# Moving the attention values, their transposes, the masking and the FFN subtractions in the issue order of a fused top-k attention and FFN kernel

## Chip, cores and metric

The kernel runs on one core of a Trainium2 chip. The metric is the device time in microseconds of one execution, as the median of several runs. The core has five engines with a queue each, and each works through its queue in order: PE (matmuls, with weight loads as PEld), DVE (vector), ACT (activations and copies), POOL (element by element), and SP, which here only issues DMAs.

## The reference, cut to what matters

```python
# q, k, v: (8, 8, 576, 64) float32
scores = np.matmul(q, k.transpose(0, 1, 3, 2)) / 8.0
kth = np.partition(scores, -32, axis=-1)[..., -32:-31]
scores = np.where(scores >= kth, scores, -1e9)
attn = np.exp(scores - scores.max(-1, keepdims=True))
attn = attn / (attn.sum(-1, keepdims=True) + 1e-09)
x = np.matmul(attn, v)                                   # back to (4608, 512)
h = x @ w_in                                             # 512 -> 2048
out = (h - np.tanh(h)) @ w_out                           # 2048 -> 512
```

So each row of 576 scores keeps its 32 largest, these go through a softmax, and the attention output feeds a two-layer network (the FFN below). w_in and w_out come as float64; the kernel converts them to float32 itself.

## The kernel before

The work is cut into 144 **steps**. A step is 128 query rows (`qt`) of a pair of heads (`hp`) of one batch (`b`), both heads `t` side by side. Four `qt` cover 512 of a batch's 576 rows; the last 64 rows of two neighbouring head pairs make a "rem" step. Steps stand in **groups** of up to two `qt` with the same heads, and what follows the softmax is done once per group. The rows of all heads together feed a **unit** of the FFN: 256 rows ("xT"), or 128 left-over rows of two batches ("xTr").

What happens to step n, and on which engine:

- `scores(n)`: matmuls (L237, PE) into the one PSUM tile `scps`, then a copy to `sc` (L245, ACT). The two heads use the two halves of the array's rows.
- `search(n, ...)`: DVE finds the 32 largest. It first merges the halves of each row (L267, L268: reads `scps` and `sc`, writes `ab`, two buffers), then takes four rounds of max and match_replace (L270 to L278). Between the rounds `between(i)` issues other DVE work: turning k and q (L222), the reciprocals of the sums (L345), the turn of an earlier `z` (L376), and pieces of the weights' conversion.
- `mask(n, ...)`: POOL makes the threshold `tb` (L294) and the bias `nb` (L303) from `m`; for each head ACT makes a Relu (L307) and POOL subtracts it from the scores (L310), which gives `z`. Last come the row checks `bad` (L314, POOL), the last readers of `ab`: they find rows in which the fast search could be wrong.
- `expo(n)`: two exponentials with their row sums (L330, ACT), then `rd` (L340, POOL).
- The probabilities have to be turned for the product with v. For the first batch this is done by `turn_pe` ("pe" steps): nine PE transposes (L409) and ACT copies to `et` (L412), eight transposes in a first part and one in a second. For all others DVE turns blocks (L376) and 16 DMAs per group on SP spread them into `et` (L390). `et` has one buffer.
- `spread(n)` copies the inverted sums to `rx` (L355, POOL).
- `values(n)`: twenty matmuls in pairs per normal group (L433, PE; the two heads use the two halves of the array's columns), then one transpose of `rx` for each step of the group (L441, PE) into the same PSUM tile `av`. ACT copies it to `xs` (L445), and POOL multiplies the two parts into the unit's `xT` (L457, or L448 for left-over rows). If this completes a unit, the unit's FFN items join the list `work`.

The FFN items are `ffn_h` (L486: x times w_in; every second one has tanh L498, copy L499 on ACT and the subtraction L500 on POOL, giving `g`) and `ffn_o` (L507: two matmuls of g times w_out; every eighth copies to `ot`, L517, and stores). The tiles `th`, `ot` and the conversion's `f` share four buffers.

The conversion of the weights (`convert`) runs in the first steps: DVE L157, L163 and L169, ACT L158, L161 and L166, POOL L172.

The order of all this is written out by hand. The loop at the end of `run` takes one pass per step n and issues, in this order: `spread(n-3)`; `values` of a group that is due (three or four steps old); `rate()`, which sets how many FFN items this pass may take from `work`; the first part of `turn_pe(n-2)`; `mask(n-1)`; `search(n)`; the DMAs of `spread_keys(n-2)`; `deal(0.4)`, which issues that share of the items; `scores(n+1)`; the second part of `turn_pe`; `expo(n-1)`; `deal(0.2)`; `values(n-2)` for pe steps; `deal(0.2)`; loads; `deal(0.2)`. After all steps the rest of `work` is issued. `rate()` spreads the items now in `work` over the passes to the next completed unit:

```python
have, low, high = len(work), 0.0, None
coming = sorted((t, u.n // 8) for u, t in ready.items() if t > n)
for t, k in coming + [(NS + 4, 0)]:
    r = have / max(t - n, 1)
    high = r if high is None else min(high, r)
    have += k
```

At the end of the kernel a flag is computed from `bad`; only if it is set does an exact second run follow. It is not executed with these inputs.

Of the kernel before, what the change touches and what calls it, by code (L numbers as in the profile page):

```python
# [8 lines left out]
AF = mybir.ActivationFunctionType  # L9
ALU = mybir.AluOpType  # L10
FP32 = mybir.dt.float32
# [5 lines left out]
BIG = 2.0**80  # L17
# [31 lines left out]
def kernel(  # L49
# [9 lines left out]
    nc = tc.nc  # L59
    P = nc.NUM_PARTITIONS  # L60
    B, H, S, D = q.shape
# [9 lines left out]
    NG = P // G  # L71
    KC = 2 * S // P
    G = 32
    NG = P // G
# [17 lines left out]
    zpool = pool("z", 2)  # L92
# [191 lines left out]
    def mask(n, exact):  # L284

        x = st[n]
        sc, m = x["sc"], x.pop("m")
        scf = sc[:].rearrange("p t s k -> p t (s k)")
        tb = mpool.tile([P, 2], FP32, tag="tb", name="tb")
        if exact:  # L290
            nc.gpsimd.tensor_scalar(tb[:], m[:, :, TOP - 1], BIG, None, ALU.mult)
        else:
            for t in range(2):
                nc.gpsimd.tensor_scalar(  # L294
                    tb[:, t : t + 1],
                    m[:, t, TOP - 1 : TOP],
                    m[:, t, TOP - 9 : TOP - 8],
                    BIG,
                    ALU.min,
                    ALU.mult,  # L300
                )
        nb = mpool.tile([P, 2], FP32, tag="nb", name="nb")
        nc.gpsimd.tensor_scalar(nb[:], m[:, :, 0], -scale, None, ALU.mult)  # L303
        z = zpool.tile([P, 2 * S], FP32, tag="z", name="z")
        zv = z[:].rearrange("p (t k) -> p t k", t=2)
        for t in range(2):
            nc.scalar.activation(  # L307
                zv[:, t, :], scf[:, t, :], AF.Relu, bias=tb[:, t : t + 1], scale=-BIG
            )
            nc.gpsimd.tensor_tensor(zv[:, t, :], scf[:, t, :], zv[:, t, :], ALU.subtract)  # L310
        if not exact:
            ab = x.pop("ab")
            for t in range(2):
                nc.gpsimd.tensor_scalar(  # L314
                    bad[:, t, n : n + 1],
                    ab[:, t, S2 + 7 : S2 + 8],
                    BIG,
                    tb[:, t : t + 1],
                    ALU.mult,
                    ALU.is_gt,  # L320
                )
        x.update(z=z, zv=zv, nb=nb)

    rds = {}
# [94 lines left out]
    def values(n):  # L419

        g = steps[n]
        nq, u = g.nq, g.unit
        et = tiles(ets.pop(n), nq)
        rx = rxs.pop(n)
        w = nq * P
        av = zt_ps.tile([P, 2, N], FP32, tag="zt", name="av")
        for i in range(2 if g.rem else 1):
            cols = half(i) if g.rem else slice(0, w)
            es = et[:, 2 * i : 2 * i + 2] if g.rem else et
            hp = g.hp + i  # L430
            for c in range(J + 1):
                for t in range(2):
                    nc.tensor.matmul(  # L433
                        av[half(t), 0, cols],
                        vb[g.b, hp][:, t, c, :] if c < J else vr[g.b, hp][:, t, :],
                        es[:, :, (J + 1) * t + c if c < J else J].rearrange("p a i j -> p a (i j)"),
                        start=(c == 0),
                        stop=(c == J),
                    )
        for i in range(nq):  # L440
            nc.tensor.transpose(  # L441
                av[:, 1, 0:w].rearrange("p (a i j) -> p i a j", a=NG, i=nq)[:, i], rx[:, i].rearrange("p t d -> p (t d)"), ident[:]
            )
        xs = xrpool.tile([P, 2, N], FP32, tag="xs", name="xs")
        nc.scalar.copy(xs[:, :, 0:w], av[:, :, 0:w])  # L445
        if g.rem:
            for i in range(2):
                nc.gpsimd.tensor_tensor(  # L448
                    xt(u)[:, g.hp + i, g.col : g.col + R],
                    xs[:, 0, half(i)],  # L450
                    xs[:, 1, half(i)],
                    ALU.mult,
                )
        else:

            xv = xs[:, :, 0:w].rearrange("p s (a i j) -> p s i a j", a=NG, i=nq)
            nc.gpsimd.tensor_tensor(  # L457
                xt(u)[:, g.hp, g.col : g.col + w].rearrange("p (i a j) -> p i a j", a=NG, i=nq),
                xv[:, 0],
                xv[:, 1],  # L460
                ALU.mult,
            )
        if n in done:
            work.extend(ffn(u))
# [6 lines left out]
            u.xT = p.tile([P, CD, N], FP32, tag=u.tag, name=u.tag)  # L471
        return u.xT

    cur = {}

    def ffn_h(u, item):

        w = u.n
        per = 2 * P // w
        for f in range(item * per, (item + 1) * per):  # L480
            j, fo = f // FJ, (f % FJ) * P
            s = f * w % 512
            if s == 0:
                cur[u] = h_ps.tile([P, 512], FP32, tag="h", name="hps")
            for c in range(CD):
                nc.tensor.matmul(  # L486
                    cur[u][:, s : s + w],
                    w_in[j][:, c, fo : fo + P],
                    u.xT[:, c, 0:w],
                    start=(c == 0),  # L490
                    stop=(c == CD - 1),
                )
        if item % 2:
            th = thpool.tile([P, 512], FP32, tag="th", name="th")
            if item % 4 == 1:
                u.g.append(gpool.tile([P, 2, 512], FP32, tag="g", name="g"))
            g = u.g[-1][:, item % 4 // 2, :]
            nc.scalar.activation(th[:], cur[u][:], AF.Tanh)  # L498
            nc.scalar.copy(g, cur[u][:])  # L499
            nc.gpsimd.tensor_tensor(g, g, th[:], ALU.subtract)  # L500

    def ffn_o(u, i, part):
        if part == 0:
            cur[u] = h_ps.tile([P, DM], FP32, tag="h", name="ops")
        for f in range(2 * part, 2 * part + 2):
            o = f * u.n + i * P
            nc.tensor.matmul(  # L507
                cur[u][:],
                u.g[o // 1024][:, o % 1024 // 512, o % 512 : o % 512 + P],
                w_out[f // FJ][:, f % FJ, :],  # L510
                start=(f == 0),
                stop=(f == CF - 1),
            )
        if part < CF // 2 - 1:
            return
        ot = thpool.tile([P, DM], FP32, tag="th", name="ot")
        nc.scalar.copy(ot[:], cur[u][:])  # L517
        for rows, dst in u.blocks[i]:
            nc.sync.dma_start(dst, ot[rows, :])
# [50 lines left out]
    def run(exact):  # L570
# [67 lines left out]
        def here(i):  # L638
            return 0 <= n + i < NS
# [24 lines left out]
        def rate():  # L664
# [8 lines that stand above are left out]
            for u, t in begun.items():  # L673
                if t > n and u in before:
                    need = [i + 1 for i, x in enumerate(work) if x[1] is before[u]]
                    if need:
                        low = max(low, need[-1] / (t - n))
            return max(low, high)
# [11 lines left out]
        for n in range(-4, NS + 4):  # L690
            pe = here(-2) and steps[n - 2].pe
            if here(-3) and not steps[n - 3].pe:
                spread(n - 3)
            for m in (n - 4, n - 3):
                if 0 <= m < NS and steps[m].last and steps[m].lag == n - m:
                    values(m)
            share, usable = rate(), converted[0]
            if pe:
                w = turn_pe(n - 2)
                next(w)  # L700
            if here(-1):
                mask(n - 1, exact)
            if here(0):
                search(n, exact, between)
            elif here(-2):
                between(0)
            if here(-2) and not pe and steps[n - 2].last:
                spread_keys(n - 2)
            if pe:
                spread(n - 2)  # L710
            deal(0.4)
            if here(1):
                scores(n + 1)
            if pe:
                next(w)
            if here(-1):
                expo(n - 1)
            deal(0.2)
            if pe and steps[n - 2].last:
                values(n - 2)  # L720
            deal(0.2)
            for fn in todo.pop(n, []):
                fn()
            deal(0.2)
# [48 lines left out]
```

## Time and profile before

| what | value |
|---|---|
| median of 5 runs | 1547.95 us (1546.23 to 1551.09) |
| the profiled execution's own time | 1551.75 us |
| its span in the profile | 1549.9 us |
| PE busy | 1442.3 us, 93% |
| DVE busy | 1347.3 us, 87% |
| ACT busy | 883.1 us, 57% |
| POOL busy | 941.4 us, 61% |
| granted PE clock, mean | 0.975 |

The page cuts the span into 40 slices and shows each engine's busy share in tenths and the granted clock of PE likewise. A group row names line, engine, operation, tiles and shape, then the time in all and the mean of one. A timeline row gives start, length of a merged run of equal instructions, engine, line, operation, and in brackets the idle time ahead and what ended it. A row of waits says who waited for whom: microseconds in total, times, longest. A row of stretches gives each engine's busy time in a window, with instructions in brackets, then clock, DMA share and rate. Ends of matmuls are modelled, and matmuls overlap; the distance from the start of one to the start of the next is measured.

### The profile page before, as it was taken

What the parts mean: (1) busy time and instruction counts of PE and PEld (TensorE: products, weight loads), DVE (VectorE), ACT (ScalarE), POOL (GpSimd) and SP (SyncE); (2) the same over time, 40 slices, a digit from 0 to 9 for tenths busy, and PEclk for the clock granted to TensorE, in tenths of its full rate; (3) what the DMA queues carried; (4) which work ended last, traced back from release to release, by engine and by line L of the source; (5) the groups of instructions that cost most, each with busy time, mean ns of one, the idle gap of its engine ahead of it and who ended that gap; (6) DMA issues with size and microseconds to landing.
All of it is one profiled execution on the core that took longest, in us unless ns stands there. A gap on an engine that the chain in (4) does not pass through costs nothing.

```text
span 1549.9 us, 25298 instructions
## 1 busy us (share of the span) xinstructions
PE 1442.3 (93%) x7428; PEld 913.1 (59%) x7428; DVE 1347.3 (87%) x3828; ACT 883.1 (57%) x1567; POOL 941.4 (61%) x1525
## 2 busy tenths in 40 slices
PE   2566899899999999999999999999999999999997
PEld 1355467456565665656565665656566665656673
DVE  7987889999999999999999999999999999997300
ACT  4886767556565565656555565656565565655320
POOL 3777667667565675657565675757565675746420
PEclk9777899999999999999999999999999999999999
DMA  9944113324443354334443354234443345322200
GB/s 248 361 167 157 50 28 66 91 69 93 106 92 76 82 105 103 70 79 95 103 89 76 81 105 103 70 79 97 102 89 80 81 99 110 81 64 59 73 10 16
DMA packets 258835, 147.42 MB, mean 95 GB/s; under 512 B 210048, under 2 KB 217216, under 8 KB 258688
## 3 DMA queue, kind: packets, MB, share of 16 engines
q1 hardware_dynamic: 256912, 145.49, 38.4%
q8 instruction: 62, 1.02, 0.3%
q14 instruction: 85, 0.70, 0.2%
q10 hardware_dynamic: 1776, 0.22, 0.1%
HBM read 61.85 MB, written 9.44 MB: 46 GB/s over the span
## 4 chain that ended last, share of the span: by engine, by line
PE 73%; DVE 10%; SPq 5%; ACT 4%; issue 3%; DMA 2%; POOL 2%; DVEq 0%; ACTq 0%; POOLq 0%
PE ops L507 28%; PE hps L486 26%; PE av L433 9%; PE scps L237 8%; SPq L390 4%; DVE m L275 3%; DVE ab L278 3%; PE av L441 2%; SPq L200 2%; ACT z L307 1%; PE zt L409 1%; DVE ab L270 1%; ACT sc L245 1%; DVE spare L376 1%; ACT f L158 1%
## 5 line engine op out<-in xcount | busy, mean ns | idle before, releaser
L507 PE MATMUL ops<-w_out,g 128*128 128x512 f32 x1152 | 525.3, 602 | 0.0
L486 PE MATMUL hps<-xT,w_in 128*128 128x256 f32 (+1 forms) x2176 | 474.3, 373 | 1.2 <-POOL xT L457 1.2
L275 DVE MAX8 m<-ab 128x8 f32<-128x288 f32 (+1 forms) x1152 | 463.0, 442 | 0.0
L310 POOL TENSOR_TENSOR z<-sc,z 128x576 f32<-128x576 f32 x288 | 400.1, 1412 | 84.4 <-ACT z L307 84.4
L486 PEld LDWEIGHTS hps<-xT,w_in 128*128 128x128 f32 x2176 | 393.1, 194 | 73.4 <-issue 20.2
L278 DVE MATCH_REPLACE8 ab<-m,ab 128x288 f32<-128x288 f32 x864 | 375.2, 441 | 0.0
L507 PEld LDWEIGHTS ops<-w_out,g 128*128 128x128 f32 x1152 | 212.0, 192 | 243.6 <-issue 240.0
L307 ACT ACTIVATE z<-sc,tb 128x576 f32<-128x576 f32 x288 | 207.6, 769 | 152.8 <-POOL tb L294 152.8
L500 POOL TENSOR_TENSOR g<-g,th 128x512 f32<-128x512 f32 x144 | 183.9, 1277 | 123.1 <-ACT g L499 111.1
L245 ACT COPY sc<-scps 128x1152 f32<-128x1152 f32 x144 | 160.9, 1117 | 116.5 <-PE scps L237 112.6
L330 ACT ACTIVATE z<-z,nb 128x576 f32<-128x576 f32 x288 | 221.5, 773 | 6.8 <-POOL z L310 6.7
L237 PE MATMUL scps<-kT,qT 64*128 64x288 f32 (+1 forms) x1280 | 185.0, 438 | 29.4 <-DVE qT L222 26.7
L433 PE MATMUL av<-et,vb 128*64 128x256 f32 (+1 forms) x1088 | 131.7, 377 | 45.4 <-ACT et L412 37.8
L237 PEld LDWEIGHTS scps<-kT,qT 64*128 64x128 f32 (+1 forms) x1280 | 100.2, 181 | 121.8 <-issue 58.4
L267 DVE TENSOR_TENSOR ab<-scps,sc 128x576 f32<-128x576 f32 x144 | 107.5, 746 | 73.5 <-POOL bad L314 58.4
L498 ACT ACTIVATE th<-hps 128x512 f32<-128x512 f32 x144 | 85.4, 593 | 108.1 <-PE hps L486 105.7
L457 POOL TENSOR_TENSOR xT<-xs 128x256 f32<-128x256 f32 (+1 forms) x68 | 47.3, 695 | 161.1 <-ACT xs L445 160.9
L445 ACT COPY xs<-av 128x512 f32<-128x512 f32 (+1 forms) x84 | 44.1, 525 | 164.8 <-PE av L441 164.7
L433 PEld LDWEIGHTS av<-et,vb 128*64 128x64 f32 x1088 | 74.7, 138 | 104.2 <-ACT et L412 39.8
L340 POOL TENSOR_SCALAR rd<-den 128x2 f32<-128x2 f32 x144 | 33.4, 232 | 146.9 <-ACT z L330 104.8
L270 DVE MAX8 ab<-ab 128x8 f32<-128x288 f32 x288 | 116.3, 444 | 0.0
L268 DVE TENSOR_TENSOR ab<-scps,sc 128x576 f32<-128x576 f32 x144 | 107.3, 745 | 0.0
(67 smaller groups left out, 1248.8 us busy)
## 6 DMA issues: line engine op xcount, KB each, us to landing
et<-spare SPq DMA_DIRECT2D x448, 72.0 KB, 2.0
et<-zx SPq DMA_DIRECT2D x448, 72.0 KB, 2.0
kin<-in_k_dram SPq DMA_DIRECT2D x116, 72.0 KB, 2.4
vb<-in_v_dram SPq DMA_DIRECT2D x64, 128.0 KB, 2.5
out_dram<-ot SPq DMA_DIRECT2D x32, 256.0 KB, 2.2
qin<-in_q_dram SPq DMA_DIRECT2D x113, 72.0 KB, 2.3
w_out<-in_moe_w_in_dram SPq DMA_DIRECT2D x10, 512.0 KB, 5.5
w_out<-in_moe_w_in_dram SPq DMA_DIRECT2D x10, 511.5 KB, 6.0
```

The source lines that it names most:

```text
L237: nc.tensor.matmul(ps[rows, t, s, 0:S2], qT[g.b, g.hp + i][half(t), qs], kT[g.b, g.hp + i][half(t), ks], start=True, stop=True,)
L245: nc.scalar.copy(sc[:], ps[:, :, :, 0:S2])
L270: nc.vector.max(ab[:, t, S2 : S2 + 8], lo[:, t, :])
L275: nc.vector.max(m[:, t, m8], last[t] if i == rounds - 1 else cur[t])
L278: nc.vector.match_replace(nxt[t], m[:, t, m8], cur[t], NEG)
L307: nc.scalar.activation(zv[:, t, :], scf[:, t, :], AF.Relu, bias=tb[:, t : t + 1], scale=-BIG)
L310: nc.gpsimd.tensor_tensor(zv[:, t, :], scf[:, t, :], zv[:, t, :], ALU.subtract)
L330: nc.scalar.activation(x["zv"][:, t, :], x["zv"][:, t, :], AF.Exp, bias=x["nb"][:, t : t + 1], scale=scale, accum_out=den[:, t : t + 1],)
L433: nc.tensor.matmul(av[half(t), 0, cols], vb[g.b, hp][:, t, c, :] if c < J else vr[g.b, hp][:, t, :], es[:, :, (J + 1) * t + c if c < J els ...
L486: nc.tensor.matmul(cur[u][:, s : s + w], w_in[j][:, c, fo : fo + P], u.xT[:, c, 0:w], start=(c == 0), stop=(c == CD - 1),)
L500: nc.gpsimd.tensor_tensor(g, g, th[:], ALU.subtract)
L507: nc.tensor.matmul(cur[u][:], u.g[o // 1024][:, o % 1024 // 512, o % 512 : o % 512 + P], w_out[f // FJ][:, f % FJ, :], start=(f == 0), sto ...
```

## The change

Four things move, and nothing is added or left out of the computation.

1. `mask`: the row checks come ahead of the Relus and subtractions.
2. The FFN's subtraction is no longer issued in `ffn_h`. It is kept in a list and issued by `finish()`: once in each pass, right after `mask(n-1)`, and ahead of the first `ffn_o` of a block.
3. `mask(n-1)` comes ahead of the first part of `turn_pe(n-2)`, whose ACT copies are L412.
4. `values` becomes a generator in two parts. For a group that is not "pe", the transposes come first, after `deal(0.4)` and ahead of `scores(n+1)`; the matmuls and all that follows come right after `scores(n+1)`. `rate()` is called in the same place as before, which is now ahead of them. For pe steps values and transposes keep their order and place.

```diff
@@ mask
         nc.gpsimd.tensor_scalar(nb[:], m[:, :, 0], -scale, None, ALU.mult)
-        z = zpool.tile([P, 2 * S], FP32, tag="z", name="z")
-        (the loop with the Relu and the subtraction)
         if not exact:
             ab = x.pop("ab")
             (the two row checks)
+        z = zpool.tile([P, 2 * S], FP32, tag="z", name="z")
+        (the loop with the Relu and the subtraction)
@@ values
         av = zt_ps.tile([P, 2, N], FP32, tag="zt", name="av")
+        def repeat_sums():
+            for i in range(nq):
+                nc.tensor.transpose(...)
+        if not g.pe:
+            repeat_sums()
+        yield
         (the matmuls)
-        for i in range(nq):
-            nc.tensor.transpose(...)
+        if g.pe:
+            repeat_sums()
@@ ffn_h, ffn_o
-    cur = {}
+    cur, unfinished = {}, []
+    def finish():
+        for g, th in unfinished:
+            nc.gpsimd.tensor_tensor(g, g, th[:], ALU.subtract)
+        unfinished.clear()
-            nc.gpsimd.tensor_tensor(g, g, th[:], ALU.subtract)
+            unfinished.append((g, th))
     def ffn_o(u, i, part):
         if part == 0:
+            finish()
@@ the loop of run
-            for m in (n - 4, n - 3):
-                if 0 <= m < NS and steps[m].last and steps[m].lag == n - m:
-                    values(m)
             share, usable = rate(), converted[0]
+            if here(-1):
+                mask(n - 1, exact)
+            finish()
             if pe:
                 w = turn_pe(n - 2)
                 next(w)
-            if here(-1):
-                mask(n - 1, exact)
...
             deal(0.4)
+            due = [values(m) for m in (n - 4, n - 3)
+                   if 0 <= m < NS and steps[m].last and steps[m].lag == n - m]
+            for x in due:
+                next(x)
             if here(1):
                 scores(n + 1)
+            for x in due:
+                next(x, None)
             if pe:
                 next(w)
...
             if pe and steps[n - 2].last:
-                values(n - 2)
+                for _ in values(n - 2):
+                    pass
```

## The prediction, made before the changed kernel was run

> **What bounds the kernel now.** I read the page's slices first, then stretches of the span, the order of the matrix engine (PE), and what each engine waits for.
>
> ```profile
> PE   2566899899999999999999999999999999999997
> ...
> DVE  7987889999999999999999999999999999997300
> ...
> PEclk9777899999999999999999999999999999999999
> ```
>
> Three regimes: up to about 200 us PE is half idle at 0.7 of its clock; then both engines are full; from 1450 us PE works alone. The stretches, cut at starts of score blocks, separate the middle:
>
> ```profile
> core 0: us, PE busy (x) PEld busy (x) DVE busy (x) ACT busy (x) POOL busy (x), PEclk, DMA share, GB/s
> 250.30:447.70 197.40, 186.34 (x931) 117.99 (x930) 196.19 (x560) 115.11 (x205) 129.79 (x214) 0.99 0.39 88
> 447.70:1432.90 985.20, 983.00 (x5007) 610.46 (x5006) 924.60 (x2626) 563.56 (x992) 627.27 (x1039) 1.00 0.38 87
> 1432.90:1549.90 117.00, 106.71 (x461) 68.00 (x460) 12.35 (x31) 26.24 (x49) 27.00 (x34) 0.97 0.13 33
> ```
>
> Stretch A (to 447.7) is DVE's: 196 of 197 us. Stretch B (to 1432.9) is PE's: 983 of 985, and DVE has 60 us over. Stretch C is a PE tail. So in B and C what counts is PE's own time, and PE's starts show what it pays for order:
>
> ```profile
> 801.07 3.60 PE L507 MATMUL ops<-w_out,g 128*128 128x512 f32 x8
> 804.59 1.24 PE L237 MATMUL scps<-kT,qT 64*128 64x288 f32 x8
> 805.76 3.70 PE L507 MATMUL ops<-w_out,g 128*128 128x512 f32 x8
> 809.39 1.95 PE L433 MATMUL av<-et,vb 128*64 128x256 f32 x16
> 811.17 0.60 PE L433 MATMUL av<-et,vr 128*64 128x256 f32 x4
> 811.70 0.44 PE L441 MATMUL av<-ident,rx 128*128 128x128 f32 x2
> 811.98 1.02 PE L507 MATMUL ops<-w_out,g 128*128 128x512 f32 x2
> ```
>
> Eight `ops` matmuls take 8 x 0.429 = 3.43 us start to start inside a block. Before scores they take 3.52, between scores and values 3.63. The third column group of a PE row (64\*128, 128\*128, 128\*64) is the shape in which the array is used, and every change of it shows 0.09 us of drain ahead and a slower first instruction or pair behind. The single starts in this window give the latter: 0.533 us to the second instruction for the usual 0.429 entering `ops`, 0.348 for 0.242 (a pair, both halves at once) entering scores, 0.267 for 0.216 entering values, 0.164 for 0.109 entering the transposes. One change thus costs 0.20 into scores or the FFN, 0.145 into values, 0.15 into transposes. With that a row of prices is complete, and block by block it gives the steps of B as the trace has them: scores 1.17 with both ends, values 2.31, two transposes 0.28.
>
> **The values.** Before, a group pays FFN-scores 0.20, scores-FFN 0.20, FFN-values 0.145, values-transposes 0.15 = 0.69 us; transposes and FFN share a shape. After, the transposes join the FFN ahead of the scores (nothing), then transposes-scores, scores-values, values-FFN. At every switch the next start lies 0.07 before the modelled end of the last record (592 to 523, 403 to 332, 379 to 310 ns), so a transpose of 273 ns hands over after 0.20, 0.09 over its 0.109. That gives 0.20 (into scores) + 0.14 (into values) + 0.20 (into the FFN) = 0.54: 0.15 saved. The built order has 67 groups directly behind scores (the 14 of the first batch keep their place, three stand in the tail without scores, +0.05 each): 67 x 0.15 - 0.15 = **9.9 us** less PE work. Scores-values is a change the trace lacks: bounds nothing (0.14 less) and both changes through the full array (0.34, 0.20 more); I take one change, 0.09 + 0.05, its nearest rows. The Trainium skill (TensorEngine Tiling (Array Packing), Key Properties) says that changing the mode, not merely the tile, drains the array; by it this is one drain, as taken, while its neighbourly placement saves nothing of it.
>
> **The FFN moves too.** `rate()` still runs at the top of the step, but the finished unit's work now joins the list after it, so that step deals less. In the built order FFN matmuls (0.216, 0.112, 0.429 us each) sum to 127.5 us in A before and 118.8 after, 707.5 and 707.6 in B, 96.9 and 105.5 in C. So 8.6 us slide from A to the tail. With scores, values and switches, PE's own work is A 183.4 -> 170.8, B 981.8 -> 975.9, C 106.3 -> 115.0.
>
> **Running sum.** Scores n+1 start at the later of PE's earlier work and 1.47 us after search n began (it reads the one PSUM buffer; 1.44 to 1.5 at every blocked step). A search starts at the later of DVE's last work and 2.55 us after its scores started (the least shown, usual in B). Starting from 256.3 (search at A's beginning), A's twenty searches hold 184.2 us of DVE work, less 1.6 of overlap between them: last search 438.9, next scores 440.4, against 447.7. Before, it came late because PE itself stood still, in its values above all (PE's waits in A: total, times, longest):
>
> ```profile
> PE av L433 <- DMA et<-zx: 3.3, 2, 1.7
> PE av L433 <- DMA et<-spare: 2.7, 2, 1.9
> ...
> PE av L433 <- DMA qin<-in_q_dram: 2.0, 1, 2.0
> ```
>
> So DVE is A's bound after the change without a gap, and PE idles 19.3 us there, in steps that were dealt two or three FFN items. These waits of values on their DMAs cost nothing then: PE has the time. B: PE's 975.9 exceed the 925.4 that DVE needs, and step by step only 0.4 is lost: 440.4 + 975.9 + 0.4 = 1416.7 against 1432.9. C: 1416.7 + 115.0 = **1531.7, against 1539.2** for PE's end: -7.5. Left out are waits that may return: B lost 3.4 before (first FFN matmuls waiting for xT, L457), and A's lulls leave PE idle up to 3.9 us in a step. I add 3. After the 2 us wait near 376 the granted clock of 370 to 380 us was 0.83, half clock for 3.4 us, or 1.7 lost; this is inside those 3. The skill (TensorE: Matmul & The Clock Gate, Why this matters for your kernels) warns of gaps over some 3 us, which speaks against A's lulls; by its threshold the three steps of A with over 3 idle would each pay 1.7, as far as DVE does not cover it; the row shows it at 2 us already.
>
> **Masking and row checks, up to 250 us.** PE's order stays there.
>
> DVE's waits from 0 to 250 us, then ACT's from 60 to 180 (total, times, longest):
>
> ```profile
> DVE f L169 <- ACT f L161: 16.0, 4, 5.0
> ...
> DVE ab L267 <- POOL bad L314: 5.4, 3, 2.8
> ```
>
> ```profile
> ACT et L412 <- PE zt L409: 13.8, 12, 3.9
> ```
>
> DVE sets the pace here, for PE has gaps in every slice. The L169 and the L412 waits belong together: ACT stands before the L412 copies for PE's transposes, with ready masking (L307, two of 0.72) behind, then conversion (L158), for which DVE waits. At 101.95 ACT waited 3.95 with tb finished at 104.4; masking first uses 1.25 of it. Four such waits: -5 (no more than 4 x 1.44 = 5.8). Opposite: where transposes are ready first, copies now wait for tb, some 0.5 in five earlier steps, and the last subtractions (1.27) run ahead of POOL's L172: +3 together. Row checks move ahead of two 1.4 us subtractions: the 5.4 shrinks by 0.75, 1.7 (scores' copy ends 202.8, then) and about 0.8, -3. Sum **-5**, bounds -11 (5.8 and all of the 5.4) to +4 (neither, the 3, and one more for row checks ahead of the subtractions). All of it reaches the end, since DVE has no wait from 214 to 363 us and A inherits the shift. Behind 448 us the same check wait is 51.7 us but DVE has that room: nothing.
>
> **Deferred FFN subtractions** (1.28 each, POOL 61% busy) no longer hold tb behind PE. th has four buffers, a step makes at most three; the first g is read by `ops` eight items after its last. Nothing. **Covers of the moved values:** the transposes waited for rx 6.0 us in all; now they run about 4 later. Values hold the one `et`, so the 16 DMAs of the next group start some 3.6 later on SP (10 us of issue each 18.8; loads behind them are five steps early), but their reader is later too. ACT's xs copy now stands between scores' copy and the exponentials: 2.31 values + 0.53 copy + 0.17, less the 1.2 scores' copy, is 1.8 us; DVE's turn of z starts 2.2 or more after them in B. 0.4 remains.
>
> **Sum:** -7.5 + 3 - 5 = -9.5. The profiled execution took 1551.75 us (span 1549.9 and 1.85 around it): 1542.2. It is 3.8 above the median of 1547.95; there the forecast is **1538.5**.
>
> **Rivals.** Each price is laid on the forecast. (1) *Scores-values costs two changes*: 0.20 x 67 = 13.4 of work, 11.0 by the running sum as A belongs to DVE: 1549.5. For: weights of values span both row halves. Against: every switch shown pays once. (2) *Exponentials late*, the slower side: if the delay on ACT passes 2.2 us, DVE's turn waits. With an excess of 0.5 us a group the running sum gives +9.3 (no change within the bound of the forecast), with 0.75 it is +16.8: A's 10 groups pay 7.5 in full, and of B's room of 50 us, 0.9 for each of 57 groups, so much is missing where two groups come close that 9.3 is paid. That is **1555**; from some 0.6 on the kernel is slower. For: 0.4 margin. Against: exponentials still end 5.8 after scores' start, the turn comes at 6.2. (3) *The early part loses*: copies waiting for tb and L172 behind subtractions cost the +4 that bounds it, -7.5 + 3 + 4 = -0.5: 1547.5, no change. (4) *The early chain shortens wholly*, -11, and no leftover wait: 1529.5. For: ACT, PE and POOL wait for each other in a ring there, so that a gain may come round again. Against: the ring runs at half clock half of the time.
>
> **Chances.** Forecast 0.62, (4) 0.10, (1) 0.07, (3) 0.06, (2) and other losses 0.15. 0.2% (3.1 us) is about what a measurement can tell: faster 0.72, same 0.13, slower 0.15. Range 1530 to 1552: from (4) to just past (1), with the edge of (2).
>
> **What would show it.** Values' start 1.17 us behind scores', their first pair 0.267; 67 fewer gaps. First scores after A near 435 (447.7 before), tail of 115. DVE's check wait below 10 us; L169's near 11. If DVE waits for L330 at L376, rival 2; if the values' first start is over 1.3 behind, rival 1.

## The result and the profile after

| | before | after |
|---|---|---|
| median | 1549.68 us (55 runs, 1546.23 to 1552.42) | 1550.77 us (32 runs, 1548.12 to 1555.33) |
| profiled execution, span | 1551.75, 1549.9 us | 1551.99, 1550.2 us |
| start of stretch A | 250.3 | 253.0 |
| end of A, end of B | 447.7, 1432.9 | 442.4, 1424.9 |
| end of PE's last matmul | 1539.8 | 1540.4 |

The ratio is 1.0011, 95% interval 1.0005 to 1.0016: no change by the prediction's own bound of 0.2%, where 9.5 us less were forecast. (PE's last end is taken here with the modelled end of the record; the running sum of the prediction counts it 0.6 lower, 1539.2.) After's lines are numbered on: values L443, their transposes L430, `xs` L453, FFN L499 and L521, the FFN's subtraction L486 (in `finish`), Relu L318, masking's subtraction L321, row checks L307. Up to L278 and in the conversion the numbers are those of before.

The slices of the page look much as before; what differs is mostly too small for tenths:

```profile
PE   2565899889999999999999999999999999999997
...
DVE  6998899999999999999999899999999899888100
```

The stretches, cut again at starts of score blocks, tell more (columns as before):

```profile
core 0: us, PE busy (x) PEld busy (x) DVE busy (x) ACT busy (x) POOL busy (x), PEclk, DMA share, GB/s
253.00:442.40 189.40, 176.71 (x870) 111.87 (x869) 189.10 (x541) 111.89 (x199) 123.34 (x209) 0.97 0.40 89
442.40:1424.90 982.50, 978.62 (x5047) 625.30 (x5046) 926.36 (x2644) 560.57 (x998) 629.15 (x1042) 1.00 0.39 88
1424.90:1550.20 125.30, 115.40 (x481) 71.99 (x480) 12.35 (x31) 26.15 (x49) 28.72 (x36) 0.97 0.12 31
```

A is 8.0 us shorter, B 2.7, the tail is 8.3 longer, and A starts 2.7 later. A is DVE's (189.1 of 189.4). B is not quite PE's any more: it lasts 982.5 against a forecast PE work of 975.9, so 6.6 us are left over. PE's order in B shows the values where they were put:

```profile
799.83 0.27 PE L430 MATMUL av<-ident,rx 128*128 128x128 f32 x1
800.04 1.24 PE L237 MATMUL scps<-kT,qT 64*128 64x288 f32 x8
801.21 1.95 PE L443 MATMUL av<-et,vb 128*64 128x256 f32 x16
802.99 0.60 PE L443 MATMUL av<-et,vr 128*64 128x256 f32 x4
803.52 7.17 PE L499 MATMUL hps<-xT,w_in 128*128 128x256 f32 x32
```

Values start 1.17 behind scores and last 2.31: one change is paid at each border, as priced, and the FFN follows at once. What PE waits for in B, and at a wait of values:

```profile
PE ops L521 <- POOL g L486: 2.2, 2, 1.2
PE av L443 <- DMA vb<-in_v_dram: 1.6, 1, 1.6
```

```profile
594.00:597.40 3.40, 3.40 (x5) 1.32 (x6) 2.49 (x9) 1.89 (x5) 1.86 (x7) 0.50 0.72 121
```

The second view is a stretch that begins 0.85 us behind the end of the wait for `vb` (591.5 to 593.15): clock 0.50 for 3.4 us, so 1.7 lost. With 2.2 and 1.6 this is 5.5 of the 6.6 us that B holds above PE's work.

In the early part the waits of DVE (0 to 250 us) are less than before, as forecast:

```profile
DVE f L169 <- ACT f L161: 12.3, 5, 4.1
...
DVE ab L267 <- ACT sc L245: 4.4, 5, 1.7
```

L169's is 12.3 where 16.0 stood (near 11 forecast), and the 5.4 for the row checks is gone. Still A begins 2.7 late. The time is not in DVE's waits; it is in DVE's busy time. Up to the start of A, before and then after (columns as above, DVE's is the third):

```profile
0.00:250.30 250.30, 166.21 (x1036) 116.64 (x1036) 214.14 (x613) 178.15 (x322) 157.28 (x240) 0.86 0.53 162
```

```profile
0.00:253.00 253.00, 166.91 (x1037) 117.65 (x1037) 222.21 (x614) 177.84 (x322) 154.50 (x241) 0.89 0.53 160
```

DVE is busy 8.1 us longer and idle 5.4 shorter, which is the 2.7. Two timelines show where the busy time comes from, before and then after, the same stretch of the conversion (DVE's L163 writes the mantissas, L169 joins sign and exponent, POOL's L172 is the product):

```profile
57.55 0.41 DVE L163 TENSOR_SCALAR w_in<-w_out 128x512 uint32<-128x512 uint32 x1
58.28 1.26 POOL L172 TENSOR_TENSOR w_in<-w_in,f 128x512 f32<-128x512 f32 x1
```

```profile
58.64 1.31 POOL L172 TENSOR_TENSOR w_in<-w_in,f 128x512 f32<-128x512 f32 x1 [0.20 <-DVE f L169]
58.75 1.48 DVE L163 TENSOR_SCALAR w_in<-w_out 128x512 uint32<-128x512 uint32 x1
```

Before, L163 is through when the product starts, and takes 0.41. After, the row checks no longer stand ahead of the product on POOL, the product starts 0.11 ahead of L163, and L163 takes 1.48: it ends 0.28 us behind the product's end. I call such an instruction **held**. Before has no held L163 of 32, after seven, 7.5 us above the median together. Over L157, L163 and L169 together, before has 12 held instructions and after 18, 7.5 and 14.9 us above the medians: 7.4 of the 8.1. (Held means here over one and a half times the median of its line.) All held L157 and L163 of both executions end 280 to 288 ns after the end of a POOL instruction, all held L169 546 to 554 ns. The Trainium skill (SBUF — State Buffer, SBUF: two separate sides) says that GpSimd and certain DVE instructions share a pair of ports under an exclusive lock, so that whoever starts second blocks until the other's whole instruction is over; these ends agree with it.

Not every DVE instruction beside POOL is held, and the trace has its own comparison for that. For the first 16 pieces L169 reads its second input `e` from PSUM, for the last 16 from SBUF (where `e` is `f`, the tile that it also writes). Two of before, each half a microsecond into a product:

```profile
60.27 2.61 POOL L172 TENSOR_TENSOR w_in<-w_in,f 128x512 f32<-128x512 f32 x2 [0.72 <-ACT e L161]
60.80 0.66 DVE L169 SCALAR_TENSOR_TENSOR f<-w_out,e 128x512 uint32<-128x512 uint32 x1
...
97.57 1.26 POOL L172 TENSOR_TENSOR w_out<-w_out,f 128x512 f32<-128x512 f32 x1 [0.94 <-DVE f L169]
98.09 1.29 DVE L169 SCALAR_TENSOR_TENSOR f<-spare,f 128x512 uint32<-128x512 uint32 x1
```

In before and in after, eight L169 with `e` in PSUM began inside a two-input POOL instruction that had over 0.3 us to go, and none was held; of those with it in SBUF, ten in before and eight in after began so, and all were held.

### The profile page after: what moved, and what is told of

Same layout as the page of the kernel before. It is cut to its first block, busy times and chain, and to the rows that moved or that the text cites. A ratio compares the mean times of both kernels' runs of the same rounds, so it can differ in the third digit from the quotient of the medians.

```text
span 1550.2 us, 25250 instructions
## 1 busy us (share of the span) xinstructions
PE 1437.6 (93%) x7428; PEld 926.8 (60%) x7428; DVE 1350.0 (87%) x3828; ACT 876.5 (57%) x1567; POOL 935.7 (60%) x1525
## 4 chain that ended last, share of the span: by engine, by line
PE 76%; DVE 11%; ACT 3%; SPq 3%; POOL 2%; issue 2%; DMA 2%; DVEq 0%; POOLq 0%; ACTq 0%
PE hps L499 30%; PE ops L521 27%; PE av L443 9%; PE scps L237 8%; DVE m L275 3%; DVE ab L278 3%; SPq L200 2%; PE av L430 1%; SPq L390 1%; DVE f L169 1%; DVE spare L376 1%; PE zt L409 1%; DVE ab L268 1%; DVE ab L267 1%; ACT et L412 1%
## 5 line engine op out<-in xcount | busy, mean ns | idle before, releaser
L521 PE MATMUL ops<-w_out,g 128*128 128x512 f32 x1152 | 521.3, 603 | 2.2 <-POOL g L486 2.2
L499 PE MATMUL hps<-xT,w_in 128*128 128x256 f32 (+1 forms) x2176 | 467.8, 373 | 0.1
L321 POOL TENSOR_TENSOR z<-sc,z 128x576 f32<-128x576 f32 x288 | 400.5, 1414 | 104.8 <-ACT z L318 104.7
L499 PEld LDWEIGHTS hps<-xT,w_in 128*128 128x128 f32 x2176 | 395.9, 194 | 69.1 <-issue 20.7
L278 DVE MATCH_REPLACE8 ab<-m,ab 128x288 f32<-128x288 f32 x864 | 375.5, 442 | 0.0
L521 PEld LDWEIGHTS ops<-w_out,g 128*128 128x128 f32 x1152 | 213.8, 191 | 260.6 <-issue 249.8
L318 ACT ACTIVATE z<-sc,tb 128x576 f32<-128x576 f32 x288 | 208.0, 772 | 106.5 <-POOL tb L294 106.4
L486 POOL TENSOR_TENSOR g<-g,th 128x512 f32<-128x512 f32 x144 | 181.9, 1283 | 30.2 <-ACT g L512 24.9
L443 PE MATMUL av<-et,vb 128*64 128x256 f32 (+1 forms) x1088 | 134.9, 385 | 33.4 <-ACT et L412 33.4
L443 PEld LDWEIGHTS av<-et,vb 128*64 128x64 f32 x1088 | 75.6, 142 | 85.9 <-ACT et L412 35.8
L294 POOL TENSOR_SCALAR tb<-m 128x1 f32<-128x1 f32 x288 | 84.9, 302 | 24.9 <-DVE m L275 19.1
```

What stands on the lines that cost most here:

```text
L278: nc.vector.match_replace(nxt[t], m[:, t, m8], cur[t], NEG)
L318: nc.scalar.activation(zv[:, t, :], scf[:, t, :], AF.Relu, bias=tb[:, t : t + 1], scale=-BIG)
L443: nc.tensor.matmul(av[half(t), 0, cols], vb[g.b, hp][:, t, c, :] if c < J else vr[g.b, hp][:, t, :], es[:, :, (J + 1) * t + c if c < J els ...
L499: nc.tensor.matmul(cur[u][:, s : s + w], w_in[j][:, c, fo : fo + P], u.xT[:, c, 0:w], start=(c == 0), stop=(c == CD - 1),)
L521: nc.tensor.matmul(cur[u][:], u.g[o // 1024][:, o % 1024 // 512, o % 512 : o % 512 + P], w_out[f // FJ][:, f % FJ, :], start=(f == 0), sto ...
```

## The experiments

Theory at the outset: the values' move gives what was priced, but hands back 8.6 us in the tail, since `rate()` no longer sees the unit that has just been finished; the other three edits lose at the start. Rival: the values' place is itself worth nothing. The table has the stretches of one profiled execution each (start of A, end of A, end of B, end of PE's last matmul), and the ratio to runs of before on the same chip. The executions that were profiled lie within 2.7 us of their kernels' medians, but for e1 and e3, which took 3.9 and 4.8 us more; their stretches are to be read with that in mind.

| kernel | start | A ends | B ends | PE ends | median (runs) | ratio, 95% |
|---|---|---|---|---|---|---|
| before | 250.3 | 447.7 | 1432.9 | 1539.8 | | |
| after | 253.0 | 442.4 | 1424.9 | 1540.4 | 1550.77 (32) | 1.0011 [1.0005, 1.0016] |
| e1 after, share told | 255.1 | 452.0 | 1428.5 | 1535.4 | 1540.56 (8) | 0.9946 [0.9926, 0.9965] |
| e2 values alone | 250.2 | 442.8 | 1423.4 | 1539.0 | 1551.06 (12) | 1.0011 [1.0002, 1.0019] |
| e3 the other three alone | 256.6 | 453.1 | 1437.8 | 1544.8 | 1551.57 (11) | 1.0011 [1.0002, 1.002] |
| e4 after, masking put back | 264.6 | 455.2 | 1436.1 | 1551.6 | 1562.15 (5) | 1.0077 [1.0064, 1.009] |
| e5 values, share told | 250.7 | 446.9 | 1424.1 | 1531.1 | 1541.92 (6) | 0.9953 [0.9935, 0.997] |
| e6 e5 + row checks first | 257.0 | 451.1 | 1427.6 | 1534.5 | 1544.71 (10) | 0.9969 [0.996, 0.9979] |
| e7 e5 + deferred subtractions | 256.1 | 450.8 | 1428.1 | 1535.0 | 1545.40 (9) | 0.9977 [0.9966, 0.9988] |
| e8 e5 + masking first | 247.5 | 445.8 | 1423.0 | 1530.0 | 1537.72 (5) | 0.9923 [0.991, 0.9935] |
| e9 e8, transposes behind values | 247.0 | 445.7 | 1421.8 | 1528.7 | 1540.60 (6) | 0.9938 [0.9918, 0.9957] |
| e10 before without L172 | 242.1 | 438.7 | 1423.7 | 1530.7 | 1542.47 (5) | 0.9963 [0.995, 0.9976] |
| e11 after without L172 | 248.0 | 438.6 | 1418.1 | 1533.7 | 1543.52 (6) | 0.9965 [0.9953, 0.9977] |
| e12 e6, mantissas earlier | 259.1 | 456.4 | 1432.8 | 1539.7 | 1546.98 (11) | 0.9991 [0.9982, 1.0] |
| e13 e8, mantissas earlier | 255.5 | 452.6 | 1429.8 | 1536.8 | 1543.03 (11) | 0.9964 [0.9952, 0.9975] |
| e14 e6, most mantissas earlier | 253.0 | 448.6 | 1425.0 | 1531.9 | 1540.57 (6) | 0.9940 [0.9926, 0.9954] |
| e15 e8, most mantissas earlier | 247.6 | 443.1 | 1420.4 | 1527.3 | 1537.23 (6) | 0.9924 [0.9905, 0.9943] |

### e1: the share told of the unit that is due

```diff
-        def rate():
-            have, low, high = len(work), 0.0, None
+        def rate(soon):
+            have, low, high = len(work) + len(soon), 0.0, None
...
-            credit = min(credit, 1.0)
+            if work or not soon:
+                credit = min(credit, 1.0)
...
-            share, usable = rate(), converted[0]
+            soon = [item for m in (n - 4, n - 3) if 0 <= m < NS and steps[m].lag == n - m
+                    and m in done for item in ffn(steps[m].unit)]
+            share, usable = rate(soon), converted[0]
```

> The changed kernel, except that the rule for the shares counts the FFN items of the unit that the step is about to finish, as the kernel before did; values, transposes, masking and subtractions stay where the change put them. Theory P (postponed FFN): the switches save their 10 us on PE, and 8.6 us of FFN that slid from stretch A to the tail give them back. Then A has 179 us of PE work instead of 171, the tail some 106 instead of 115, and the time is 5 to 8 below the changed kernel: 1543 to 1546. Rival V (values behind scores cost as much elsewhere as they save): the tail shrinks, but the last scores come later by as much, and the time stays within 2 of 1550.8.

It took 1540.56, more gain than expected. The tail went from 115.5 to 106.9 (PE's end less B's), and B held 0.6 above PE's work where after held 6.6. The one edit takes both away, so both come from the list that is filled later: passes in A are dealt few FFN items and PE idles there (a **lull**), and the items are left for the tail. By which steps it leads to the waits in B was not traced.

### e2, e3 and e4: which part costs

e2 is before with the values' part of the diff alone. e3 is after with that part undone. e4 is after with one edit undone:

```diff
-            if here(-1):
-                mask(n - 1, exact)
-            finish()
             if pe:
                 w = turn_pe(n - 2)
                 next(w)
+            if here(-1):
+                mask(n - 1, exact)
+            finish()
```

> The kernel before with the values and transposes moved and nothing else: masking, row checks and FFN subtractions stand as before. Theory P: the first 250 us are those of the kernel before (scores block at 250.3, not 253.0), the tail is 115, the PE waits for FFN subtractions (2.2 us, ops behind g) are gone, so about 2 to 4 below the kernel before: 1546 to 1548, if the row checks' wait on DVE costs nothing. Rival V: not faster than before, 1550 to 1552.

> The changed kernel with values and transposes put back: only masking, row checks and FFN subtractions are moved. Theory P: the start is 2.7 us late as in the changed kernel (253.0 at the block that stood at 250.3), no switch is saved, the tail is 106, DVE's wait for row checks is gone but was covered: 1551 to 1553. Rival V: the moved values are what made the start late too, so the first 250 us are those of before: 1548 to 1550.

> The changed kernel, except that the first part of the PE turn stands ahead of the masking again, as before. Theory P, for the start: ACT then copies turned weights while tb is still on its way (0.86 us of wait in each of the conversion steps 2 to 5 goes), so the block at 253.0 returns to 250 or earlier, and the time falls by 2 to 5: 1546 to 1549. Rival D (the deferred FFN subtractions ahead of the weights' product on POOL make the start late): no change, 1550 to 1551.

e2 missed its time (1551.06), which is the one that rival V gave: the stretches moved as expected up to B's end, but the lull takes what the switches give. That it is the lull and not the values' place is settled by e5 below. e3 fits in its time; the other three edits alone make the start 6.3 us late, more than the 2.7 expected. e4 was a plain miss, by some 15 us and in sign: with masking behind the turned weights' copies A starts 11.6 later than in after. So putting masking first helps, and the loss at the start must come from the row checks or the deferred subtractions. ACT's waits from 60 to 180 us, in e4 and in after, say how:

```profile
ACT et L412 <- PE zt L409: 13.1, 10, 4.0
```

```profile
ACT z L318 <- POOL tb L294: 6.3, 7, 1.2
...
ACT et L412 <- PE zt L409: 4.3, 3, 1.7
```

This is the pair of waits that the prediction named, 13.8 before: ACT stood before L412 for PE with masking ready behind; now it waits less for PE and some for `tb`. The other two edits can be read together as well: e4 has them, e2 has not, and nothing else parts these kernels. The start is 14.4 later in e4, the median 11.1 higher.

### e5: the values' part with the share told

Before with the values' part of the diff and e1's edit.

> The kernel before with the values and transposes moved and the share rule told of the unit that is due; masking, row checks and FFN subtractions as before. Theory P + C (C: the late start is DVE's conversion instructions, L163 above all, that stand still while POOL works through its subtractions or products; the reordered POOL work of the change met them seven times, before none): start as before (250.2), no stretched L163, the gain of the first experiment kept, so 4 to 5 below its 1540.6: 1535 to 1538. Rival B (the row checks' wait on DVE, 52 us before, was no free cover once PE is shorter): 1541 or more.

The profiled span is 1538.2; the median, 1541.92, lies above what was expected and in rival B's range. But rival B's reason does not show: DVE still waits 30.2 us for row checks in B, and PE waits there for 0.5 us in all. Against e2, which differs only in e1's edit, the median is 9.1 lower and PE ends 7.9 earlier (the profiled span is 10.4 shorter; the other 2.5 lie behind PE's last matmul). What PE waits for in B has shrunk to this:

```profile
PE hps L499 <- POOL xT L465: 0.3, 1, 0.3
PE scps L237 <- DVE ab L268: 0.2, 1, 0.2
```

### e6, e7 and e8: the other three, one at a time on e5

e6 has the row checks ahead of the Relus and subtractions; e7 has `unfinished.append((g, th))` and `finish()`, called behind the first part of `turn_pe`; e8 has `mask(n - 1)` ahead of that part.

> As e5_values_share, and the row checks ahead of the subtractions. Theory C says the row checks' move alone pushes the subtractions and products on POOL by 1.1 us onto L163: some seven stretched L163 (1.48 for 0.41 us), the block of 250.2 at 254 to 260, time 4 or more above e5. Rival M (the masking's new place makes it): start as in e5.

> As e5_values_share, and the FFN subtractions deferred. Steps 2 to 5 have no FFN work, so there no change; from step 6 on POOL's products come 1.28 later. Theory C: L163 not stretched, a few L157 may be; start within 2 of e5, and time within 3 of e5 (waits of ops for g add 2). Rival D (the deferral makes the late start): start 4 or more later than e5.

> As e5_values_share, and masking ahead of the turned weights' copies, alone of the change's moves on ACT and POOL. My prediction's step for the masking gave -5 and +3: start 2 to 5 earlier than e5, if POOL's products stay clear of L163. Theory C: what counts is the stretched instructions; masking earlier by some 0.7 us moves the subtractions the other way than the row checks do, so few are stretched, and the time is at or below e5. Rival M: start later than e5 by 3 or more.

Row checks first: start +6.3, median +2.8, a smaller loss than expected, with seven held L163 where e5 has none. Deferral: start +5.4, median +3.5, where theory C said within 2 and 3: rival D's start. Masking first: start -3.2, median -4.2, as expected. The intervals of e5 overlap with those of e6 and e7 and touch that of e8, so the sizes are rough; those of e7 and e8 are far apart. DVE's busy and idle time up to the start of A tells the three apart (e14 comes below):

| us | before | after | e5 | e6 | e7 | e8 | e14 |
|---|---|---|---|---|---|---|---|
| DVE busy | 214.14 | 222.21 | 214.25 | 223.35 | 218.43 | 217.45 | 220.28 |
| DVE idle | 36.16 | 30.79 | 36.45 | 33.65 | 37.67 | 30.05 | 32.72 |

Against e5 the row checks add 9.1 of busy time and take 2.8 of idle time, the deferral adds 4.2 and 1.2, and masking first adds 3.2 and takes 6.4. In e7 POOL has the FFN's subtractions ahead of `rx` (L355), and PE's transposes in the first batch wait longer for it, 10.7 us with one of 2.8, where e5 has 6.0 and 1.8:

```profile
PE av L430 <- POOL rx L355: 10.7, 6, 2.8
```

### e9: the transposes behind the values again

```diff
-        if not g.pe:
-            repeat_sums()
         yield
...
-        if g.pe:
-            repeat_sums()
+        repeat_sums()
```

> The kernel of e8_mask_share (values moved, share rule told, masking ahead of the turned copies), but the sums' transposes stand behind the values again: scores, values, transposes, FFN. As many changes of the array's shape as before, three a group, but the FFN enters from the transposes for nothing and the transposes cost 0.15 where values-FFN cost 0.20: PE's work in stretch B 973.3 for 975.8. By the switch prices the time falls by 2 to 3: 1535. Rival: the transposes ahead of the scores gave room for the xs copy, whose delay now holds the exponentials and DVE's turn of z, and the time rises above 1538.

Inconclusive: PE ends 1.3 earlier in the profile, the median is 2.9 higher, the intervals overlap. What the transposes' place is worth is not settled; it is small beside the other parts.

### e10 and e11: the product on POOL left out

```diff
-        nc.gpsimd.tensor_tensor(dst, dst, f[:], ALU.mult)
```

> The kernel before without POOL's product in the conversion of the weights (L172; the weights keep their mantissas alone, so the FFN's numbers are others). It is the baseline for the next. No L169 is held by a product any more (five of ten were); the start is a few us earlier than before: block of 250.3 at 243 to 249.

> The changed kernel without POOL's product in the conversion of the weights (L172, as in e10). Theory C: the seven stretched L163 were all held by that product, so none is left, and the start is no longer later than in e10, but 0 to 4 us earlier, as the masking's new place gives. The tail and the lull stay: the time is 1 to 5 below e10. Rival M (row checks and deferral cost POOL's queue, whatever DVE meets): the start stays 3 to 6 later than in e10.

A miss for the expectation that without the product both start alike: e11 starts 5.9 later than e10. But six L163 and seven L157 are held in e11 still, now mostly by masking's subtraction (L321 in after), which follows earlier on POOL; one L157 takes 4.40 us, until two such subtractions and one of the FFN, back to back, are over. Taking away one holder puts another in its place, so this did not separate holding from a mere longer queue on POOL.

### e12 and e13: the held instruction moved out of the way

L163 of a piece is issued ahead of L169 of the piece before it, so that it is through when that piece's product starts. e12 does this to e6, e13 to e8.

```diff
+        if soon_ok(piece):
+            low_bits()
+        yield
         hi = raw[:, :, 1]
...
-        nc.vector.tensor_scalar(dst.bitcast(U32), shifted[:, :, 0], 0x0FFFFFFF, None, ALU.bitwise_and)
+        if not soon_ok(piece):
+            low_bits()
```

> The kernel of e6 (values alone with the share told, and the row checks ahead of the Relus and subtractions), with DVE's mantissa instruction (L163 in after) of most weight pieces issued earlier: ahead of L169 of the piece before it, so that POOL's product of that piece (L172) is not yet running. Nothing is left out. e6 began stretch A at 257.0 with seven stretched L163 (20.8 us in all), e5 at 250.7 with none. Theory H (DVE's instruction is held while POOL's product runs, and this is what the row checks made late): hardly any stretched L163, stretch A begins at 250 to 253, PE's end 1530 to 1532, time 1540 to 1542.5. Rival Q (the row checks only lengthen POOL's queue, and the stretched instructions are a symptom beside it): stretch A still begins at 254 to 257, time 1543 to 1546.

> The kernel of e8 (values alone with the share told, and masking ahead of the turned weights' copies) with the same earlier mantissa instructions as e12. Nothing is left out. e8 began stretch A at 247.5, with four stretched L163 (18.2 us in all against 13.3 with none) and 1537.7 us. Theory H: 2 to 4 us less at the start, stretch A from 243.5 to 246, time 1533.5 to 1536.5. Rival Q: within 1 us of e8 in both.

Both missed and were slower than e6 and e8. The instruction now came ahead of its data: DVE waited for two loads (L157 here is after's L163):

```profile
DVE w_in L157 <- DMA w_out<-in_moe_w_in_dram: 3.9, 1, 3.9
DVE w_out L157 <- DMA spare<-in_moe_w_out_dram: 3.6, 1, 3.6
```

Between these two, in searches 3 to 9, e12 had gained: 102.1 us where e6 took 107.3 and e5 99.3. The time by which DVE's conversion instructions exceeded their medians in these searches was 9.9, 13.6 and 5.3.

### e14 and e15: the same without the two load waits

```diff
     def soon_ok(piece):
-        return piece < WJ * CD or piece % CD > 1
+        return 6 <= piece < 31 and (piece < WJ * CD or piece % CD > 1)
```

> The kernel of e12, but the first six weight pieces and the last keep their mantissa instruction in its old place, since in e12 DVE stood 3.9 us (piece 3) and 3.6 us (piece 31) before this instruction for a load that had not landed. Nothing is left out. In searches 3 to 9, between those two waits, e12 took 102.1 us, e6 107.3 and e5 99.3; the lengthening of held DVE instructions over their medians in the same searches was 9.9, 13.6 and 5.3. Theory H (held DVE instructions are what the row checks cost): searches 3 to 9 stay near 102, and without the two load waits stretch A begins at 251 to 254, PE's end 1530 to 1532.5, time 1540.5 to 1543. Rival Q (only POOL's longer queue counts): stretch A at 256 to 258, time 1544 to 1546.

> The kernel of e13 with the same seven mantissa instructions back in their old place. Nothing is left out. Theory H: like e8 or 1 to 3 us ahead of it, stretch A from 244.5 to 247.5, time 1535 to 1537.7. Rival Q: within 1 us of e8's 1537.7. If it is later than e8 by over 1.5 us, the moved instruction takes DVE's time in a place where the masking step needs it, and e8 stays the best version.

e14 came out as theory H said: searches 3 to 9 take 102.7, A starts at 253.0 (e6: 257.0), the median is 1540.57 (e6: 1544.71), and the intervals are disjoint. In the stretch shown above, L163 (here L157) runs at 56.79, well ahead of the product (here L183), and takes 0.44:

```profile
56.79 0.44 DVE L157 TENSOR_SCALAR w_in<-w_out 128x512 uint32<-128x512 uint32 x1
...
58.46 1.44 POOL L183 TENSOR_TENSOR w_in<-w_in,f 128x512 f32<-128x512 f32 x1
```

So of the 6.3 that the row checks cost at the start 4.0 came back, 3.1 of it in DVE's busy time, with five L163 held still. With the 9.1 of e6 this makes holding the larger part of their cost. What the earlier mantissas do to e5, which has no held L163, was not run. e15 is equal to e8, and H's gain at its start is not there (247.6): its conversion instructions are held 11.5 us in all and e8's 10.7, and in searches 3 to 5 L157 (here L169) is now held for as long as L163 was. e8 and e15 are the best versions, 0.8% below before and after.

## Why the prediction was wrong

That the time stayed where it was is a cancellation: A and B gave back 10.7 us, the start and the tail took 11.3. The forecast of PE's end was 10.1 us too early: change of -9.5, measured +0.6. By its own terms: the start 7.7 later than forecast (-5 forecast, +2.7 measured), A 0.7 shorter than forecast (-7.3, -8.0), B 6.2 longer (-8.9, -2.7), the tail as forecast (+8.7, +8.6), less the 3 that were added for waits.

- **The step that failed** is "Masking and row checks, up to 250 us ... Sum -5", with "Deferred FFN subtractions ... Nothing" beside it. It counted waits that shrink, and they did shrink. It took the busy time of DVE as fixed. Its part on masking (-5 + 3) was right in sign and too small: on e5 -3.2 at the start and -4.2 in time, and with the other edits in place (e4 to after) -11.6 and -11.4. Its "-3" for the row checks was +6.3 at the start and +2.8 in time (e6), and the "Nothing" of the deferral was +5.4 and +3.5 (e7). What DVE's busy time took more was +8.1 in after, +9.1 in e6 and +4.2 in e7. For the deferral it also read a row wrongly: the 6.0 us that transposes wait for `rx`, set down as covered, all lie in the first batch, whose transposes keep their place; there they became 13.3 in after. The three do not add: together they made the start 6.3 late in e3, 4.8 in e1 and 2.7 in after's profile, against +8.5 as a sum.
- **B's leftover** was mis-sized: 6.6 above PE's work where 0.4 and 3 in all were allowed. e1 and e5 show that it comes from the later list of FFN items: told of the unit that is due, B holds 0.6 and 1.4. The 3.4 that B lost before were put down to `xT`, but PE's waits there show 0.6 for `xT`, and 1.4 in one wait of values for a DMA into `et`.
- **The price of a switch** was right: 1.17 to values, 2.31 of values, tail 115; in B, work and the 5.5 us above give the measured length to about 1 us. So rival (1) is out.
- **"The FFN moves too"** was right in its 8.6 us, and in that they come back in the tail. What was not asked is whether the move is needed: a count of the unit that is due takes it away and is worth 9.1 us (e2 to e5), about as much as the whole forecast.
- **The values' part alone** (-7.5 + 3) gave -0.8 at PE's end in e2 and no gain in the medians.
- Rival (2) did not appear: DVE has no wait for the exponentials in B. Rival (3), the early part loses, is nearest to what happened, in its place and its 1547.5; but its means (copies waiting for `tb`, the product behind the subtractions) were only part: on DVE the price stands as busy time, most of it in held instructions.

Open: what makes the deferral's +5.4. On DVE it is 4.2 of busy time, as much as its held time grew (4.1), and 1.2 of idle time; but one search alone, with held instructions and the wait for `rx` both in it, is 4.2 longer, and no run takes these two apart.

## What to carry to other kernels

A wait table shows no loss that is booked as busy time: when an edit reorders one engine, compare the durations of equal instructions on the engine beside it, not only its waits. Letting a short DVE instruction run ahead of the POOL product that would hold it was worth 4.0 us at the start in e14, and nothing in e15, where another instruction was held in its place; so count all held instructions, not those of one line. And when a step moves behind the point at which a scheduler counts its work, tell the scheduler, or the gain is handed back in the tail.

## What the runs showed of the hardware

A DVE instruction of 0.415 us took up to 4.40 us beside POOL (e11), and the trace shows it as busy; in before and after the end of such a held instruction came 280 to 288 ns after POOL's (546 to 554 ns for L169, 0.678 us when free). L169 was held only where its second input lies in SBUF, never where it lies in PSUM.

A PE wait of 1.65 us in B was followed by half clock for 3.4 us (594.0 to 597.4). The Trainium skill (TensorE: Matmul & The Clock Gate, Why this matters for your kernels) puts the limit for such gaps at about 3 us; here the measurement decides, and 1.65 us was enough this once. The length of a wait alone does not decide, though: the clock was 1.00 for 5.9 us and more behind a wait of 1.88 us in before (it ended at 274.01) and one of 2.68 us in after (278.02). In after's record of the clock the half-clock stretches of A and B begin at 297.06, 331.19, 423.35 and 594.02. That is 34.13, 92.16 and 170.67 us apart, 10, 27 and 50 times 3.413, so where a wait falls on such a grid may count; no run here tests that.
